# First loads in longer rows, and a new order of the transform jobs, in a Winograd convolution with batch norm

## The chip, the cores and the metric

One core of a Trainium2 chip runs the kernel. Its engines work side by side from queues of their own: TensorE (PE, with its weight loads PEld), VectorE (DVE), ScalarE (ACT), GpSimd (POOL), SyncE (SP), and 16 DMA engines that serve the DMA queues of SP and ScalarE. The metric is the device time of one execution in microseconds (us), as a median over runs.

## What is computed

Two images `x` of 2048 positions and 1024 channels are convolved along the positions with three taps, then normalised by channel and put through silu:

```python
xp = pad(x, one position on each side)
y = sum(einsum('bsc,cd->bsd', xp[:, k:k+2048], w[k]) for k in range(3))
y = silu((y - mean) * (g / sqrt(var + 1e-5)) + b)
```

All inputs and the output are bfloat16.

## The kernel before, in words

**The method.** It is a Winograd convolution: six outputs come from eight positions. Each image is cut into frames of 126 new positions (128 rows with the overlap), 16 whole ones and a short one of 48 rows. The host lays `x` out by image `bi`, block `ct` of 128 channels, row, frame and channel, so that a block is 128 rows (partitions) of 16 frames of 128 channels: 4 KB a row, 512 KB a block, eight blocks an image. The host also cuts `w` into eight groups `dc` of 128 output channels; a group has, by row, three taps of 8 x 128 values, 2 KB each.

**Stage one: transforms ("jobs").** A matmul with a frame as the loaded weights and the constant matrix `rm` (128 x 168, eight points of 21 tiles) as the moving operand transforms one frame (line 242). `Jobs.do` (237) takes 6, 6 and 4 frames of a block as three jobs; 48 jobs cover both images, in the order image, block. The results go into two banks of PSUM, and are copied to `T_sb` as bfloat16 by ScalarE (265) or VectorE (267). `do_short` (251) does the short frames of an image in one go. Below, jobs are numbered from 1 to 48 as they are issued; job 25 is the first of image 1.

**What orders it.** `ORDER` (29) is written out by hand, token by token. A capital letter is a job, and says into which two banks it goes (A 4 and 5, B 6 and 7, C 2 and 3, D 0 and 1). Small letters say which engine copies: `d` VectorE, `a` ScalarE, one letter for the whole job, two for a bank each. `s6a` is the short job into bank 6, copied by ScalarE. A bare number is so many end products: matmuls of the points 0 and infinity of the first unit (weight group 0, image 0), which use taps 0 and 2 as loaded and collect in banks 2 and 3. `p7` is so many of that unit's inner products, which use transformed weights `u`; they collect in banks 0 and 1. `m1a` makes a multiple of a tap on ScalarE; `+` issues one of the combinations on VectorE that are kept back. `COPIES` (34) says which engine copies each of the first unit's products out of PSUM. Both kinds of products are line 415; those of the later units are line 295.

**Weights.** GpSimd makes the transformed weights of a group: sums `e` (135) and then six tiles `u` (148). For group 0 it also needs three multiples (0 and 1 of the taps 2 and 0, 2 of the middle tap 1); those that have no `m` token, GpSimd makes itself (127), `FirstWeights` (165) keeps the order.

**Stage two.** 15 further units (dc, bi) run the eight products each over 342 tiles, 64 matmuls, with combinations on VectorE and silu on ScalarE. The last unit is cut in halves to shorten the end.

**Loads.** `load_x` (97) and `load_w` (105) issue from SP's queue. There are six buffers for blocks of `x`, so block 6 waits until the matmuls of block 0 are done, and so on. The program also lets each load wait for the landing of the load eight before it. In before, blocks 0 and 1 of image 0 and block 0 of image 1 come in halves by frames: 128 rows of 2 KB each. Of blocks 0 and 1 of image 0, the second half is issued from ScalarE's queue, behind `rm`. The parameters `prm` (541) are issued third from SP, and GpSimd works out scale and beta from them (217) before its first sum. Taps 0 and 2 of group 0 lie apart in the tile and come in two loads, tap 1 in a third.

Of the kernel before, what the change touches and what calls it, by code (L numbers as in the profile page):

```python
# [13 lines left out]
P = 128  # L14
# [12 lines left out]

BANKS = {"A": 4, "B": 6, "C": 2, "D": 0}
ORDER = (
    "Dda Bad Dda Cad Aad s6a Dda Cda Ada Dda 5 m1a 1 Bad Aad Da Bda Ada 2 Bda Dad Aad 1 Ba Dda 1 Ada 1 "  # L30
    "Bd 1 Dda Ada Bda 1 m2a 1 Dad Ada Ba 2 p7 Ada Cad Ba p1 Aad p3 Cad p1 Ba p1 Ada Cad p3 Bad p1 Ada p1 "
    "Cda p1 Ba p6 + Ada + p2 Cad p1 Bad Aad p2 s2a Bda p1 Ada + Cad Ba Aa"
)
COPIES = {0: "d", 7: "d", 1: "d", 3: "a", 2: "a", 5: "a"}

@with_exitstack
def kernel(
# [9 lines left out]
    nc = tc.nc  # L47
# [46 lines left out]
    def load_small(bi):  # L94
        nc.sync.dma_start(out=small[bi * SROW:bi * SROW + LROWS], in_=xl[bi])

    def load_x(bi, ct, parts=1, second=nc.scalar):
        t = xpool.tile([P, NF, P], BF16, name="xw")
        xt[bi, ct] = t
        step = NF // parts  # L100
        for q in range(parts):
            s = slice(q * step, (q + 1) * step)
            (second if q else nc.sync).dma_start(out=t[:, s], in_=x[bi, ct, :, s])

    def load_w(dc, taps):
        if dc not in raw:
            raw[dc] = wpools[dc // 2 % 2].tile([P, 3, CT, P], BF16, name=f"wch{dc // 2 % 2}")
        if len(taps) == 3:
            nc.sync.dma_start(out=raw[dc], in_=w[dc])
        else:  # L110
            for k in taps:
                nc.sync.dma_start(out=raw[dc][:, k], in_=w[dc, :, k])

# [6 lines left out]
    def scaled(src, by, eng):  # L122
        t = spool.tile([P, CT, P], BF16, name="w1x2")
        if eng is nc.scalar:
            nc.scalar.mul(t, src, by)
        else:
            eng.tensor_scalar(t, src, by, 0.0, op0=ALU.mult, op1=ALU.add)
        return t

    def double_w(dc, eng):  # L130
        double[dc] = scaled(raw[dc][:, 1], 2.0, eng)

    def even(dc, q, a, b):
        sums[dc, q] = epool.tile([P, CT, P], FP32, name=f"e{q}")
        nc.gpsimd.tensor_tensor(sums[dc, q], a, b, op=ALU.add)  # L135

    def even_vector(dc, q):
        w0, w2 = raw[dc][:, 0], raw[dc][:, 2]
        sums[dc, q] = e = epool.tile([P, CT, P], FP32, name=f"e{q}")
        f, h = (w2, w0) if q == 1 else (w0, w2)  # L140
        nc.vector.scalar_tensor_tensor(out=e, in0=f, scalar=4.0, in1=h, op0=ALU.mult, op1=ALU.add)  # L141

    def transform_w(dc, q, signs=(0, 1)):
        o = double[dc] if q else raw[dc][:, 1]
        if (dc, q) not in wts:
            wts[dc, q] = upool.tile([P, 2, CT, P], BF16, name=f"u{q}")
        for i in signs:
            nc.gpsimd.tensor_tensor(wts[dc, q][:, i], sums[dc, q], o, op=(ALU.add, ALU.subtract)[i])  # L148

    def prepare_w(dc):  # L150
        even(dc, 0, raw[dc][:, 0], raw[dc][:, 2])
        transform_w(dc, 0)

        def second():
            even_vector(dc, 1)
            transform_w(dc, 1)

        def third():
            even_vector(dc, 2)
            transform_w(dc, 2)  # L160

        act_work.append(lambda: double_w(dc, nc.scalar))
        dve_work.extend((second, third))

    class FirstWeights:
# [1 line left out]


        def __init__(self, dc):
            w0, w2 = raw[dc][:, 0], raw[dc][:, 2]  # L170
            self.dc, self.src, self.made = dc, ((w2, 4.0), (w0, 4.0), (raw[dc][:, 1], 2.0)), {}
            elsewhere = [int(t[1]) for t in ORDER.split() if t[0] == "m"]
            self.steps = [(None, lambda: even(dc, 0, w0, w2))]
            self.steps += [(i, lambda i=i: self.multiple(i, nc.gpsimd)) for i in (0,) if i not in elsewhere]
            self.steps += [(0, lambda: even(dc, 1, self.made[0], w0))]
            self.steps += [(i, lambda i=i: self.multiple(i, nc.gpsimd)) for i in (1,) if i not in elsewhere]
            self.steps += [(1, lambda: even(dc, 2, self.made[1], w2))]
            self.steps += [(i, lambda i=i: self.multiple(i, nc.gpsimd)) for i in (2,) if i not in elsewhere]
            self.steps += [
                (2 if q else None, lambda q=q, i=i: transform_w(dc, q, (i,)))  # L180
                for q, i in ((0, 0), (1, 0), (0, 1), (1, 1), (2, 0), (2, 1))
            ]
            self.own = [i for i in range(3) if i not in elsewhere]
# [8 lines left out]
                self.steps.pop(0)[1]()  # L192

    def prepare_second(dc):
        w0, w2 = raw[dc][:, 0], raw[dc][:, 2]

        def first():
            even(dc, 0, w0, w2)
            transform_w(dc, 0)

        def second():
            even(dc, 1, scaled(w2, 4.0, nc.scalar), w0)

        def third():
            double_w(dc, nc.scalar)
            transform_w(dc, 1)

        def fourth():
            even(dc, 2, scaled(w0, 4.0, nc.scalar), w2)
            transform_w(dc, 2)  # L210

        return first, second, third, fourth
# [66 lines left out]
    class Unit:  # L279
# [6 lines left out]
        def product(self, q, j, add, between):  # L286
            dc = self.dc
            nsl = slice(self.lo, self.hi)
            for ct in range(CT):
                between()  # L290
                if j == 0 or j == NJ - 1:
                    lhsT = raw[dc][:, 0 if j == 0 else 2, ct]
                else:
                    lhsT = wts[dc, (j - 1) // 2][:, (j - 1) % 2, ct]
                nc.tensor.matmul(  # L295
                    self.bank[q], lhsT=lhsT, rhs=T_sb[self.bi][:, ct, j, nsl],
                    start=not add and ct == 0, stop=ct == CT - 1, skip_group_check=add,
                )
# [90 lines left out]
    class First(Unit):  # L389
# [19 lines left out]
        def do(self, todo):  # L409
            j, q, add, ct = todo.pop(0)  # L410
            if j == 0 or j == NJ - 1:
                lhsT = raw[self.dc][:, 0 if j == 0 else 2, ct]
            else:
                lhsT = wts[self.dc, (j - 1) // 2][:, (j - 1) % 2, ct]
            nc.tensor.matmul(  # L415
                self.bank[q], lhsT=lhsT, rhs=T_sb[self.bi][:, ct, j, :],
                start=not add and ct == 0, stop=ct == CT - 1, skip_group_check=True,
            )
            if ct == CT - 1:
                self.behind(j, q)  # L420
# [115 lines left out]

    load_x(0, 0, 2)
    load_x(0, 1, 2)  # L540
    nc.sync.dma_start(out=prm, in_=prm_in)
    load_small(0)
    scales()
    nc.scalar.activation(dummy[:, 1:2], dummy[:, 0:1], ACT.Silu)
    for ct in range(2, CT):
        load_x(0, ct)
        if ct == 2:
            load_w(0, (0, 2))
    load_w(0, (1,))
    load_x(1, 0, 2, nc.sync)  # L550
    for ct in range(1, CT):
        load_x(1, ct)
    load_small(1)
    load_w(1, (0, 1, 2))

# [27 lines left out]
    prev = unit  # L585
    xscope.close()
    wpools.append(ctx.enter_context(tc.tile_pool(name="wpool1", bufs=2)))
    load_w(2, (0, 1, 2))
    load_w(3, (0, 1, 2))
    for i, (dc, bi) in enumerate(seq[1:-1], 1):  # L590
        unit = Unit(dc, bi, i % 2 * 4)
        also = prev.rest(quiet)
        if i == 1:
            also = [(1, second[0]), (4, second[1])] + also
        if i == 2:
            also = prev.rest(quiet, 5, 4)
        if i == 3:
            also = also + [(1, lambda: idle(act_work)), (1, lambda: idle(dve_work))]
        if i == len(seq) - 2:
            also = prev.rest(quiet, 4, 5)  # L600
        unit.run(
            quiet, also,
            2 if i == 2 else dc + 2 if bi == 1 and 0 < dc < DC - 2 else None, i == 2, i == 1, i == 3,
        )
        if bi == 0 and dc + 3 < DC:
            load_w(dc + 3, (0, 1, 2))
        prev.store(nc.sync)
        prev = unit

# [29 lines left out]
def _laid_out(np, x, w, mean, var, g, b):  # L639


    B, S, C = x.shape
    K, _, D = w.shape
    CT, DC = C // P, D // P
    NF = S // (R * WT)
    step = R * WT
    xp = np.zeros((B, step * NF + P, C), x.dtype)
    xp[:, 1:S + 1] = x
    wins = np.stack([xp[:, f * step:f * step + P] for f in range(NF)], 2)
    wins = wins.reshape(B, P, NF, CT, P).transpose(0, 3, 1, 2, 4)  # L650
    rm = np.zeros((P, NJ, WT), np.float32)
    for n in range(WT):
        rm[R * n:R * n + NJ, :, n] = np.array(_POINTS, np.float32).T
    return (
        wins,
        xp[:, step * NF:step * NF + LROWS],
        w.reshape(K, CT, P, DC, P).transpose(3, 2, 0, 1, 4),
        np.stack([var, g, mean, b]).reshape(4, DC, P).transpose(2, 0, 1),
        rm.astype(x.dtype),
    )  # L660
# [30 lines left out]
```

## Time and profile before

| | |
|---|---|
| median of 3 runs | 181.33 us (181.33 to 181.47) |
| the profiled execution, whole time | 181.66 us |
| its span, first to last instruction | 179.8 us |
| busy: PE, DVE, ACT, POOL | 97%, 85%, 62%, 76% of the span |
| TensorE's granted clock | 1.00 in every stretch |
| DMA engines busy, 0 to 4 us, 4 to 28 us | 45%, 100% or a little more |
| read from HBM, written | 14.93 MB, 9.44 MB |

The profile is one execution. In the timeline a row gives the start, the length from the first start to the last end, engine, line, operation and count; ends of matmuls are modelled, so a row of matmuls looks longer at its end than the pitch between them, and I go by starts. In the chain that ended last, pieces follow each other without overlap. In the table by stretch, the columns are the stretch, its length, the busy time of PE, PEld, DVE, ACT and POOL with the number of instructions, the granted clock, the mean busy share of the 16 DMA engines and the rate in GB/s; a share can exceed 1, because the time of a packet is counted from when it is taken up. Time to landing is from a load's issue to its completion.

### The profile page before, as it was taken

The page shows a single profiled execution, that of the slowest core. Times are in us where ns is not written, and L with a number is a line of the kernel's source. Part 1 is how long each engine was busy: PE and PEld are TensorE (multiplying, and loading weights), DVE is VectorE, ACT ScalarE, POOL GpSimd, SP SyncE. Part 2 cuts the span into 40 slices and gives each one's busy share as a digit, 9 for nine tenths or more (in the row PEclk, how much of TensorE's full clock was granted, in tenths as well). Part 3 has the DMA queues.
Part 4 walks back from the last instruction along what each step waited for, and adds up shares of the span by engine and source line. Part 5 has one row for each costly group of instructions (what it writes and reads, how often), then busy time and mean ns, then how long its engine had stood idle before and what let it go on. Part 6 is the DMA issues. An engine that isn't in the chain of part 4 may idle for free.

```text
span 179.8 us, 3538 instructions
## 1 busy us (share of the span) xinstructions
PE 173.9 (97%) x1365; PEld 123.2 (69%) x1365; DVE 152.2 (85%) x214; ACT 111.0 (62%) x195; POOL 137.4 (76%) x75
## 2 busy tenths in 40 slices
PE   7999999999999999999999999999999999999991
PEld 2868788766666666666666666666666666668890
DVE  1779997997969999999999999987979887766691
ACT  3799899968374847265645654555356554563773
POOL 2587999999997799999999999799799949000000
PEclk9999999999999999999999999999999999999999
DMA  5999992270335030823072306430303030203033
GB/s 172 371 416 412 418 382 109 66 289 0 131 97 213 0 131 0 232 79 131 0 195 115 133 0 135 175 133 0 135 0 131 0 125 10 97 34 137 0 155 107
DMA packets 7488, 24.58 MB, mean 137 GB/s; under 512 B 1104, under 2 KB 1616, under 8 KB 7472
## 3 DMA queue, kind: packets, MB, share of 16 engines
q1 hardware_dynamic: 6896, 23.74, 35.8%
q10 hardware_dynamic: 576, 0.63, 1.0%
q8 instruction: 10, 0.16, 0.4%
q14 instruction: 6, 0.05, 0.1%
HBM read 14.93 MB, written 9.44 MB: 136 GB/s over the span
## 4 chain that ended last, share of the span: by engine, by line
PE 87%; DMA 5%; DVE 4%; ACT 1%; issue 1%; DVEq 0%
PE ps L295 75%; PE ps L242 7%; DMA xw<-in_x_dram 5%; PE ps L415 3%; PE ps L84 2%; DVE ps L310 2%; DVE t L310 1%; DVE T_sb L267 1%; DVE sd L310 1%; ACT yh L314 1%; ACT T_sb L265 0%; ACT sd L424 0%; DVE zeros L82 0%; DVEq L680 0%; PE ps L256 0%
## 5 line engine op out<-in xcount | busy, mean ns | idle before, releaser
L295 PE MATMUL ps<-T_sb,u 128*128 128x342 bf16 (+2 forms) x768 | 109.4, 298 | 0.0
L295 PEld LDWEIGHTS <-u 128*128 128x128 bf16 x768 | 72.3, 97 | 32.6
L148 POOL TENSOR_TENSOR u<-e,w1x 128x1024 bf16<-128x1024 f32 x32 | 69.4, 2192 | 7.8 <-DVE e L141 7.6
L295 PE MATMUL ps<-T_sb,wch 128*128 128x342 bf16 (+2 forms) x256 | 39.5, 299 | 0.4 <-DVE ps L310 0.4
L310 DVE SCALAR_TENSOR_TENSOR t<-ps,sd 128x684 f32<-128x684 f32 (+2 forms) x49 | 37.6, 819 | 0.6
L148 POOL TENSOR_TENSOR u<-e,wch 128x1024 bf16<-128x1024 f32 x16 | 36.5, 2300 | 1.8 <-DMA wch<-in_w_dram 1.2
L314 ACT ACTIVATE yT<-ps,beta,scale 128x342 bf16<-128x342 f32 (+1 forms) x42 | 29.1, 727 | 12.6 <-PE ps L295 12.6
L295 PEld LDWEIGHTS <-wch 128*128 128x128 bf16 x256 | 24.2, 97 | 11.1 <-issue 0.5
L304 ACT COPY pc<-ps 128x342 f32<-128x342 f32 (+2 forms) x32 | 13.6, 424 | 28.2 <-PE ps L295 27.4
L267 DVE CAST T_sb<-ps 128x504 bf16<-128x504 f32 (+2 forms) x40 | 23.4, 644 | 5.4 <-PE ps L242 5.2
L265 ACT CAST T_sb<-ps 128x504 bf16<-128x504 f32 (+4 forms) x49 | 25.4, 597 | 3.8 <-PE ps L242 3.5
L310 DVE SCALAR_TENSOR_TENSOR ps<-ps,t 128x684 f32<-128x684 f32 (+2 forms) x32 | 26.5, 829 | 0.7
L310 DVE SCALAR_TENSOR_TENSOR ps<-ps,pc 128x342 f32<-128x342 f32 (+2 forms) x34 | 16.9, 496 | 10.1 <-PE ps L295 7.2
L141 DVE SCALAR_TENSOR_TENSOR e<-wch 128x1024 f32<-128x1024 bf16 x12 | 25.4, 2116 | 0.0
L242 PE MATMUL ps<-rm,xw 128*128 128x168 bf16 x256 | 23.8, 240 | 0.4 <-DMA xw<-in_x_dram 0.3
L242 PEld LDWEIGHTS <-xw 128*128 128x128 bf16 x256 | 20.0, 99 | 4.5 <-DMA xw<-in_x_dram 2.2
L135 POOL TENSOR_TENSOR e<-wch 128x1024 f32<-128x1024 bf16 x8 | 19.0, 2372 | 0.3 <-DMA wch<-in_w_dram 0.3
L314 ACT ACTIVATE yT<-t,beta,scale 128x684 bf16<-128x684 f32 x15 | 14.4, 959 | 0.0
L310 DVE SCALAR_TENSOR_TENSOR t<-ps,t 128x684 f32<-128x684 f32 (+2 forms) x17 | 13.9, 817 | 0.0
L304 ACT COPY sd<-ps 128x342 f32<-128x342 f32 (+2 forms) x16 | 6.8, 426 | 10.3 <-PE ps L295 9.3
L310 DVE SCALAR_TENSOR_TENSOR sd<-pc,ps 128x342 f32<-128x342 f32 (+2 forms) x17 | 8.2, 482 | 5.2 <-ACT sd L304 5.2
L306 ACT ACTIVATE pc<-ps 128x342 f32<-128x342 f32 (+2 forms) x16 | 7.0, 438 | 8.8 <-PE ps L295 5.3
(42 smaller groups left out, 66.7 us busy)
## 6 DMA issues: line engine op xcount, KB each, us to landing
out_dram<-yT SPq DMA_DIRECT2D x15, 576.0 KB, 2.9
xw<-in_x_dram SPq DMA_DIRECT2D x13, 512.0 KB, 7.2
wch<-in_w_dram SPq DMA_DIRECT2D x7, 768.0 KB, 5.4
xw<-in_x_dram SPq DMA_DIRECT2D x4, 256.0 KB, 6.7
wch<-in_w_dram SPq DMA_DIRECT2D x3, 256.0 KB, 4.5
xw<-in_x_dram ACTq DMA_DIRECT2D x2, 256.0 KB, 4.6
out_dram<-yh SPq DMA_DIRECT2D x1, 256.0 KB, 2.0
xl<-in_xl_dram SPq DMA_DIRECT2D x2, 96.0 KB, 5.2
```

The lines of the kernel that those rows point to most:

```text
L135: nc.gpsimd.tensor_tensor(sums[dc, q], a, b, op=ALU.add)
L141: nc.vector.scalar_tensor_tensor(out=e, in0=f, scalar=4.0, in1=h, op0=ALU.mult, op1=ALU.add)
L148: nc.gpsimd.tensor_tensor(wts[dc, q][:, i], sums[dc, q], o, op=(ALU.add, ALU.subtract)[i])
L242: nc.tensor.matmul(src[:, q // per, q % per], lhsT=xt[bi, ct][:, f + q], rhs=rm, start=True, stop=True)
L265: nc.scalar.copy(dst, src)
L267: nc.vector.tensor_copy(dst, src)
L295: nc.tensor.matmul(self.bank[q], lhsT=lhsT, rhs=T_sb[self.bi][:, ct, j, nsl], start=not add and ct == 0, stop=ct == CT - 1, skip_group_che ...
L304: nc.scalar.copy(dst, self.bank[q])
L306: nc.scalar.mul(dst, self.bank[q], by)
L310: nc.vector.scalar_tensor_tensor(out=out, in0=in0, scalar=scalar, in1=in1, op0=ALU.mult, op1=op1)
L314: nc.scalar.activation(self.yT[:, rows, self.y0:self.y0 + self.hi - self.lo], src, ACT.Silu, bias=beta[:, dc:dc + 1], scale=scale[:, dc:dc ...
L415: nc.tensor.matmul(self.bank[q], lhsT=lhsT, rhs=T_sb[self.bi][:, ct, j, :], start=not add and ct == 0, stop=ct == CT - 1, skip_group_check ...
```

## The change

- Blocks 0 and 1 of image 0 come in two parts of 64 rows of 4 KB instead of two halves by frames of 128 rows of 2 KB. Both parts of block 0 are issued from SP; of block 1 the second part comes from ScalarE's queue.
- The parameters are issued from ScalarE's queue, third there, behind `rm` and that part.
- Block 0 of image 1 comes in one transfer.
- The host lays the taps out as 0, 2, 1, so that taps 0 and 2 of group 0 come in one transfer, in rows of 4 KB. It is issued behind block 2 and the short block.
- `ORDER` is new. The first end products come after job 11 (after job 9 in before), 14 of the 16 before job 25 as in before. The multiple m1 has no token, so that GpSimd makes it; m2 comes after job 23 (after job 24 in before). Of the 48 inner products 28 come among the jobs (31 in before), and one combination (three in before); the rest of both follows behind the jobs. The short job of image 1 comes after job 45 (after job 43).
- `COPIES`: product 0 goes from VectorE to ScalarE, product 3 from ScalarE to VectorE.

```diff
 ORDER = (
-    "Dda Bad Dda Cad Aad s6a Dda Cda Ada Dda 5 m1a 1 Bad Aad Da Bda Ada 2 Bda Dad Aad 1 Ba Dda 1 Ada 1 "
-    "Bd 1 Dda Ada Bda 1 m2a 1 Dad Ada Ba 2 p7 Ada Cad Ba p1 Aad p3 Cad p1 Ba p1 Ada Cad p3 Bad p1 Ada p1 "
-    "Cda p1 Ba p6 + Ada + p2 Cad p1 Bad Aad p2 s2a Bda p1 Ada + Cad Ba Aa"
+    "Bad Aad Da Cda Bda Ad Da Bda s2d Aad Dad Bad 2 Aa Dda 1 Bda Aad 1 Dad 1 Bda 1 Aa 1 Dda 1 Bda 1 Ada "
+    "Dda Bad 1 m2a 2 Dd 2 Bda Aad Dda 2 Bad Aad p4 Ca p1 Bad p2 Aad Cda Ba p1 Ada p2 Ca p1 Bda p2 Aad p1 "
+    "Ca p1 Bda p1 Aa p1 Cd p2 Bad p5 + Cad Ba p4 s4a Ca Bda Aa"
 )
-COPIES = {0: "d", 7: "d", 1: "d", 3: "a", 2: "a", 5: "a"}
+
+W0, W2, W1 = range(3)
+COPIES = {0: "a", 7: "d", 1: "d", 3: "d", 2: "a", 5: "a"}
...
-    def load_x(bi, ct, parts=1, second=nc.scalar):
+    def load_x(bi, ct, parts=(nc.sync,)):
+
         t = xpool.tile([P, NF, P], BF16, name="xw")
         xt[bi, ct] = t
-        step = NF // parts
-        for q in range(parts):
+        step = P // len(parts)
+        for q, queue in enumerate(parts):
             s = slice(q * step, (q + 1) * step)
-            (second if q else nc.sync).dma_start(out=t[:, s], in_=x[bi, ct, :, s])
-
-    def load_w(dc, taps):
+            queue.dma_start(out=t[s], in_=x[bi, ct, s])
+
+    def load_w(dc, taps=slice(0, 3)):
         if dc not in raw:
             raw[dc] = wpools[dc // 2 % 2].tile([P, 3, CT, P], BF16, name=f"wch{dc // 2 % 2}")
-        if len(taps) == 3:
-            nc.sync.dma_start(out=raw[dc], in_=w[dc])
-        else:
-            for k in taps:
-                nc.sync.dma_start(out=raw[dc][:, k], in_=w[dc, :, k])
+        nc.sync.dma_start(out=raw[dc][:, taps], in_=w[dc, :, taps])
...
-    load_x(0, 0, 2)
-    load_x(0, 1, 2)
-    nc.sync.dma_start(out=prm, in_=prm_in)
+    load_x(0, 0, (nc.sync, nc.sync))
+    load_x(0, 1, (nc.sync, nc.scalar))
+    nc.scalar.dma_start(out=prm, in_=prm_in)
+    load_x(0, 2)
     load_small(0)
+    load_w(0, slice(W0, W1))
     scales()
     nc.scalar.activation(dummy[:, 1:2], dummy[:, 0:1], ACT.Silu)
-    for ct in range(2, CT):
+    for ct in range(3, CT):
         load_x(0, ct)
-        if ct == 2:
-            load_w(0, (0, 2))
-    load_w(0, (1,))
-    load_x(1, 0, 2, nc.sync)
-    for ct in range(1, CT):
+    load_w(0, slice(W1, W1 + 1))
+    for ct in range(CT):
         load_x(1, ct)
     load_small(1)
-    load_w(1, (0, 1, 2))
+    load_w(1)
...
-        w.reshape(K, CT, P, DC, P).transpose(3, 2, 0, 1, 4),
+        w[[0, 2, 1]].reshape(K, CT, P, DC, P).transpose(3, 2, 0, 1, 4),
```

Elsewhere the taps' places in the tile are named `W0`, `W2`, `W1` instead of 0, 2, 1; the instructions there are the same.

More of the change, by code (lines that the diff above doesn't have):

```diff
@@ L130, in double_w @@
     def double_w(dc, eng):
-        double[dc] = scaled(raw[dc][:, 1], 2.0, eng)
+        double[dc] = scaled(raw[dc][:, W1], 2.0, eng)
     def even(dc, q, a, b):
@@ L137, in even_vector @@
     def even_vector(dc, q):
-        w0, w2 = raw[dc][:, 0], raw[dc][:, 2]
+        w0, w2 = raw[dc][:, W0], raw[dc][:, W2]
         sums[dc, q] = e = epool.tile([P, CT, P], FP32, name=f"e{q}")
@@ L143, in transform_w @@
     def transform_w(dc, q, signs=(0, 1)):
-        o = double[dc] if q else raw[dc][:, 1]
+        o = double[dc] if q else raw[dc][:, W1]
         if (dc, q) not in wts:
@@ L150, in prepare_w @@
     def prepare_w(dc):
-        even(dc, 0, raw[dc][:, 0], raw[dc][:, 2])
+        even(dc, 0, raw[dc][:, W0], raw[dc][:, W2])
         transform_w(dc, 0)
@@ L169, in __init__ @@
         def __init__(self, dc):
-            w0, w2 = raw[dc][:, 0], raw[dc][:, 2]
-            self.dc, self.src, self.made = dc, ((w2, 4.0), (w0, 4.0), (raw[dc][:, 1], 2.0)), {}
+            w0, w2 = raw[dc][:, W0], raw[dc][:, W2]
+            self.dc, self.src, self.made = dc, ((w2, 4.0), (w0, 4.0), (raw[dc][:, W1], 2.0)), {}
             elsewhere = [int(t[1]) for t in ORDER.split() if t[0] == "m"]
@@ L194, in prepare_second @@
     def prepare_second(dc):
-        w0, w2 = raw[dc][:, 0], raw[dc][:, 2]
+        w0, w2 = raw[dc][:, W0], raw[dc][:, W2]
         def first():
@@ L291, in product @@
                 if j == 0 or j == NJ - 1:
-                    lhsT = raw[dc][:, 0 if j == 0 else 2, ct]
+                    lhsT = raw[dc][:, W0 if j == 0 else W2, ct]
                 else:
@@ L411, in do @@
             if j == 0 or j == NJ - 1:
-                lhsT = raw[self.dc][:, 0 if j == 0 else 2, ct]
+                lhsT = raw[self.dc][:, W0 if j == 0 else W2, ct]
             else:
@@ L587 @@
     wpools.append(ctx.enter_context(tc.tile_pool(name="wpool1", bufs=2)))
-    load_w(2, (0, 1, 2))
-    load_w(3, (0, 1, 2))
+    load_w(2)
+    load_w(3)
     for i, (dc, bi) in enumerate(seq[1:-1], 1):
@@ L605 @@
         if bi == 0 and dc + 3 < DC:
-            load_w(dc + 3, (0, 1, 2))
+            load_w(dc + 3)
         prev.store(nc.sync)
```

## The prediction

> **What bounds the kernel now.** I read the chain of work that ended last, in order of time, then TensorE's timeline, then the DMA rates by stretch and each load's time to landing.
>
> ```profile
> 4.48 2.96 PE ps L242 x28
> 7.44 0.32 PE ps L256 x8
> 7.75 1.77 PE ps L242 x20
> 9.52 0.02 issue
> 9.54 9.25 DMA xw<-in_x_dram
> 18.79 0.05 issue
> 18.84 1.40 PE ps L242 x16
> ...
> 37.51 126.54 PE ps L295 x872
> ```
>
> Columns are start, length, what. From 18.84 us on TensorE carries the chain almost alone, and 126.54/872 = 145 ns a matmul from 37.51 on leaves no gap. Ahead of that stands one load, issued at 9.54: the first half of image 1's block 0. So the run's end is set by when that block lands, plus TensorE's work, plus its gaps between there and 37.5. Nothing after 37.5 is touched by the change.
>
> The gaps after 18.84: to 37.35 (start of the pure L295 stretch) are 18.51 us. The work is 128 transform matmuls at 72.5 ns (six take 0.43 us), 50 products of L415 at 145 ns (three take 0.43), eight of L295 and 0.24 for the short block: 9.28 + 7.25 + 1.16 + 0.24 = 17.93. **0.58 us is lost.** The largest piece is visible here:
>
> ```profile
> 31.35 0.84 PE L242 MATMUL ps<-rm,xw 128*128 128x168 bf16 x6
> 32.02 0.31 PE L415 MATMUL ps<-T_sb,u 128*128 128x342 bf16 x1
> ```
>
> Six matmuls need 0.435 us, and the next starts 0.67 after them: 0.235 waiting for a bank to be copied out. (VectorE had stood 1.0 us behind ScalarE's copy of sd, by the table of waits.)
>
> The DMA rates by stretch (length, busy time of PE, PEld, DVE, ACT and POOL, clock, DMA share, GB/s):
>
> ```profile
> 1.75:3.75 2.00, 2.00 (x4) 0.76 (x3) 0.08 (x1) 1.49 (x2) 0.00 (x0) 1.00 0.76 240
> 3.75:5.75 2.00, 2.00 (x11) 1.10 (x10) 0.68 (x1) 0.26 (x1) 0.00 (x0) 1.00 1.09 359
> 7.00:8.50 1.50, 1.50 (x25) 1.18 (x23) 1.50 (x3) 1.50 (x5) 1.34 (x3) 1.00 1.03 395
> 8.50:14.50 6.00, 5.59 (x62) 4.36 (x60) 4.94 (x10) 5.64 (x12) 5.36 (x6) 1.00 1.03 415
> 25.50:27.00 1.50, 1.50 (x19) 1.26 (x17) 1.40 (x4) 1.50 (x4) 1.50 (x2) 1.00 1.03 347
> 34.75:36.75 2.00, 2.00 (x15) 1.33 (x14) 1.97 (x4) 2.00 (x4) 2.00 (x2) 1.00 0.88 292
> ```
>
> From 4 to 28 us the DMA engines are full, so a load lands when the bytes ahead of it have moved. It runs 415 GB/s on 4 KB rows, 395 where the 2 KB rows of taps 0 and 2 pass, and less in the first four microseconds.
>
> **The change, part by part.**
>
> *Block 0 of image 1 in one transfer.* Its halves were issued at 9.54 and 9.92 and took 9.3 and 9.5 us, so they land at 18.84 and 19.42. The first job needs the whole block now: **+0.58**. (Jobs on the first half covered this before.)
>
> *Rows of 4 KB.* First two microseconds of the stream: 240 GB/s with 2 KB rows. The nearest row with longer rows is the weight load that starts at 34.75, with 6 KB rows, 292 in its first two microseconds. The difference is 0.104 MB, at 415 0.25 us. From 3.75 to 5.75 it is 359 against 415, 0.11 MB or 0.27 us; in 5.25 to 5.75 (331 and 279 GB/s in its quarters) the short block and the parameters pass, which stay, and that is 0.13 of it; between 0.14 and 0.27 I take 0.20, since the parameters leave SP's queue. Taps 0 and 2 (0.52 MB) at 415 for 395: 0.06; block 0 of image 1 alike: 0.06. Sum **-0.57**; bounds 0 and -0.64, and above zero by the first rival.
>
> *Image 0's first job later.* It used frames 0 to 5, in the first 256 KB, which landed at 0.72 + 3.5 = 4.22, when the warm-up matmuls (to 4.48) still ran. Now it needs all of block 0. SP's queue had moved 0.49 MB by 4.25, and its first two loads had landed by 1.16 + 4.2 = 5.36, so I expect the start near 5. What hides it: block 3 lands at 5.67 + 5.3 = 10.97, and the nine jobs ahead of it need 48 x 72.5 ns + 0.3 = 3.8 us. Cost nothing up to two microseconds of delay.
>
> *The six end products moved behind block 3.* They filled 9.65 to 11.0. Now TensorE must do 80 transforms (5.8 us) and 14 end products (2.03) between block 3 of image 0 and block 0 of image 1: 7.83 us, where 19.42 - 10.97 = 8.45 are there. Slack 0.62. Cost nothing while the DMA gain at block 0 of image 1 isn't over 0.62 more than at block 3. Copying out in that stretch: VectorE 10 x 0.59 + 0.76 + 2 x 0.42 = 7.5, ScalarE 10 x 0.47 + 2 x 0.61 + 2 x 0.34 = 6.6, as before (pitches from neighbouring casts in the two timelines); it fits.
>
> *Queues.* SP issues the parameters no more, and one load for two taps; each issue is 0.33 to 0.43 us. The waits of SP's queue show 1.4 us until the first load (rm) landed ahead of the ninth, and that order stays: the pair of taps is still ninth. By then 1.7 MB are queued and 0.75 moved, so earlier issues gain nothing. On ScalarE one issue of 0.45 comes before its table load (2.12 to 3.40), whose first copy is due after 5: nothing. GpSimd needs the parameters for 3.05 us of scales (6.10 to 9.15) ahead of its first sum at 9.49, which waits for the taps: 0.3 us of cover. If they land later, its u tiles do, and u0 (20.35) is first read 2.3 us after block 0 of image 1: a microsecond of cover more.
>
> *The multiple m1 from ScalarE to GpSimd.* ScalarE -1.08; GpSimd +1.04, beside its 1.2 us wait for tap 1 (17.0 to 18.23): hidden to within 0.2. *m2* stands one job earlier: ScalarE reaches it 7.5 us after block 3, tap 1 lands 7.2 after (18.2): no wait.
>
> *Jobs of image 1.* Loads of the engines from block 0 of image 1 to the last job, copies and combinations included, by the same pitches (VectorE's small operations 0.42, ScalarE's 0.35, a whole job of 1008 on ScalarE 0.90):
>
> | us | TensorE | VectorE | ScalarE |
> |---|---|---|---|
> | before | 14.3 | 13.1 | 13.1 |
> | after | 13.9 | 11.4 | 13.6 |
>
> Laid out by hand, each copy 0.2 us behind its matmuls and each bank refilled when it is empty, the new order leaves TensorE two gaps, 0.04 ahead of job 35 and 0.1 where VectorE's combination waits for ScalarE's copy of sd ahead of job 46. The copies of jobs 46 to 48 end 1.4 us after the last job, beside 12 products (1.74). So 0.14 of gaps for 0.58: **-0.44**. Bounds 0 (a layout by hand sees no jitter) and -0.58.
>
> Sum: +0.58 - 0.57 - 0.44 = **-0.43**. The profiled execution took 181.66 us (span 179.8), 0.33 above the median of the runs, 181.33; I take the difference over to the median: **180.90**. A difference under 0.2%, 0.36 us, is about what a measurement of this kernel can't tell from none.
>
> **A row that speaks against it.** Where the short block of image 1 passes (48 rows, 25.5 to 27.0), the rate is 347: 0.10 MB is missing for 0.10 MB of such rows, though the engines are busy. In 5.25 to 5.5, where the other short block passes, the share is 1.63 at 331 GB/s. Transfers that span fewer rows ran at about half rate here. [...]
>
> **Rivals.**
>
> *Parts of 64 rows run at half rate* (slower). By the rows above, half of 415 is 208. Part one runs alone at a time that gave only 170 GB/s anyway (1.75 to 2.75). Then the second part of block 0 on SP and of block 1 on ScalarE's queue share the same rows 64 to 127: until about 4.95; then the first part of block 1, 0.26 MB at 208, to about 6.15, where the same bytes had moved by 5.45 before. The stream is 0.7 late: +0.58 - 0.12 - 0.44 + 0.7 = +0.72, **182.05**; all four in series, 5.0 us from 1.75 (6.8 for 5.4), make 1.4 and 182.75. It decides from the point where the stream is late at all: without the 0.45 of gain on the first four microseconds the sum is +0.02. For: the rows of the short blocks. Against: those are of 2 KB and 48 rows, and two queues can mix parts.
>
> *Copying out takes the place of the wait* (same or slower). ScalarE has 13.6 us in a stage of 13.9. One wait like the 1.0 us of VectorE in before, less the 0.3 of slack, costs 0.7: -0.43 + 0.7 = +0.27, **181.6**; with the old 0.58 of gaps **181.3**, two waits 182.6.
>
> *The slowest DMA engine* (faster). Tap 1 lands at 18.2, 2.2 us after block 7 (8.18 + 7.8 = 15.98), though 256 KB take 0.63. In 15.2 to 16.2 one packet of instructions held an engine for 6% of 16 us, 0.96 us, and every later load waits for that engine. If it comes later, block 0 of image 1 lands up to 0.96 earlier; then TensorE's 7.83 us bind, at 10.97 - 0.51 + 7.83 = 18.29 for 19.42 - 0.57 = 18.85: 0.56 more, **180.35**. Against: its time goes with the instructions done, nearly the same here.
>
> *The rows of 4 KB bring nothing*: +0.57 on the sum, +0.14, **181.5**, counted within the forecast's own spread.
>
> **Chances.** Forecast 0.42 (its own range 180.7 to 181.4; 0.27 faster, 0.13 same, 0.02 slower); slow DMA engine 0.19, all faster; copying out 0.11 (0.05 same, 0.06 slower); half rate 0.28 (0.02 same, 0.26 slower). Faster 0.46, same 0.20, slower 0.34. The range leaves out the half rate in series and the extreme of the fast side: 180.3 to 182.1.
>
> **What will show it.** Right: about 290 GB/s or more in the first two microseconds of the stream; first transform near 5; block 0 of image 1 starting at about 18.85 in one stretch; the pure L295 stretch from about 36.9. Half rate: 200 GB/s and a share over 1 in 2 to 6 us, block 3 after 11. Copying out: block 0 early, but gaps of TensorE behind ScalarE in 20 to 34. The forecast is wrong if block 0 of image 1 starts after 19.3.

## The result, and the profile after

| | before | after |
|---|---|---|
| median, runs side by side | 181.34 us | 183.08 us (182.85 to 183.49) |
| ratio after / before | | 1.0097, 95% interval 1.0076 to 1.0119 |
| the profiled execution, whole time | 181.66 us | 183.28 us |
| its span | 179.8 us | 181.2 us |
| job 25 starts | 18.84 us | 20.62 us |
| from there to the pure stretch of products | 18.51 us | 18.10 us |
| pure stretch starts | 37.35 us | 38.72 us |
| from there to the end of the span | 142.45 us | 142.48 us |

The change made the kernel slower by 1.74 us; 180.90 was forecast, and the range ended at 182.1. The line numbers fall by one in the code of the jobs: 241, 414 and 294 are what 242, 415 and 295 were.

The table splits the difference of the profiled executions. Job 25, the first of image 1, starts 1.78 us later. The stage behind it is 0.41 shorter. The rest is the same to 0.03. So all of the loss happened before 20.6 us.

The chain that ended last, in order of time (start, length, what), of the kernel after:

```profile
1.34 5.51 DMA xw<-in_x_dram
6.85 0.14 issue
6.98 5.02 PE ps L241 x44
12.00 0.32 PE ps L255 x8
12.32 1.27 PE ps L241 x16
...
20.32 0.29 PE ps L414 x2
20.61 0.02 issue
20.62 1.33 PE ps L241 x16
```

In before this chain hung on one load that was issued at 9.54. Now it begins with the first block: its second part, issued at 1.34 and landed at 6.85. From 6.98 TensorE never pauses until job 25. And its first 44 transforms take 5.02 us, 114 ns each, where those of before came 72.5 ns apart from 6.04 to 7.20. (Before began slowly too: its first 28 took 2.96 us, 106 ns each, a wait of about 0.2 us included.)

The same stretches as before, from the table by stretch (stretch, length, busy time of PE, PEld, DVE, ACT and POOL, granted clock, DMA share, GB/s), with two more that turned out to matter:

```profile
1.75:3.75 2.00, 2.00 (x4) 0.75 (x3) 0.08 (x1) 1.41 (x2) 0.00 (x0) 1.00 0.78 218
3.75:5.75 2.00, 0.72 (x2) 0.00 (x0) 0.00 (x0) 0.08 (x1) 0.00 (x0) 1.00 1.07 220
5.75:7.25 1.50, 0.27 (x4) 0.30 (x5) 0.00 (x0) 0.00 (x0) 0.00 (x0) 1.00 1.06 201
8.50:11.50 3.00, 3.00 (x24) 3.00 (x22) 2.48 (x4) 1.77 (x4) 2.54 (x6) 0.50 1.02 354
```

Two things are to be seen. Between 3.75 and 7.25 the DMA engines are full (share over 1) and yet move 220 and 201 GB/s, where before moved 359 and 380 in the same two stretches. And from 8.5 to 11.5 TensorE runs at half its clock (0.50), with 24 matmuls recorded in 3 us.

### The profile page after: what moved, and what is told of

It is laid out like the page before. It is cut to its first block, busy times and chain, and to the rows that moved or that the text cites. A ratio compares the mean times of both kernels' runs of the same rounds, so it can differ in the third digit from the quotient of the medians.

```text
span 181.2 us, 3533 instructions
## 1 busy us (share of the span) xinstructions
PE 173.6 (96%) x1365; PEld 124.4 (69%) x1365; DVE 148.9 (82%) x211; ACT 110.3 (61%) x191; POOL 139.6 (77%) x76
## 4 chain that ended last, share of the span: by engine, by line
PE 91%; DMA 3%; DVE 3%; ACT 1%; SPq 0%; issue 0%; DVEq 0%
PE ps L294 74%; PE ps L241 12%; PE ps L414 5%; DMA xw<-in_x_dram 3%; DVE ps L309 2%; DVE t L309 1%; ACT yh L313 1%; SPq L106 0%; PE ps L255 0%; DVEq L678 0%; DVE sd L309 0%; PE ps L612 0%; DVEq L309 0%
## 5 line engine op out<-in xcount | busy, mean ns | idle before, releaser
L147 POOL TENSOR_TENSOR u<-e,w1x 128x1024 bf16<-128x1024 f32 x32 | 70.4, 2223 | 6.3 <-DVE e L140 4.9
L147 POOL TENSOR_TENSOR u<-e,wch 128x1024 bf16<-128x1024 f32 x16 | 35.7, 2249 | 0.6
L266 DVE CAST T_sb<-ps 128x504 bf16<-128x504 f32 (+3 forms) x37 | 22.9, 665 | 8.3 <-PE ps L241 7.4
L241 PE MATMUL ps<-rm,xw 128*128 128x168 bf16 x256 | 24.5, 246 | 2.5 <-DMA xw<-in_x_dram 2.5
L241 PEld LDWEIGHTS <-xw 128*128 128x128 bf16 x256 | 21.2, 102 | 5.9 <-issue 3.7
L140 DVE SCALAR_TENSOR_TENSOR e<-wch 128x1024 f32<-128x1024 bf16 x12 | 22.0, 1835 | 0.0
L134 POOL TENSOR_TENSOR e<-wch 128x1024 f32<-128x1024 bf16 x8 | 20.0, 2495 | 0.2 <-DMA wch<-in_w_dram 0.2
```

The lines of the kernel that those rows point to most:

```text
L241: nc.tensor.matmul(src[:, q // per, q % per], lhsT=xt[bi, ct][:, f + q], rhs=rm, start=True, stop=True)
L266: nc.vector.tensor_copy(dst, src)
```

## The experiments

The first theory was that the parts of 64 rows move at half rate, and that the late stream alone sets the end. The rivals were that the late first job and the clock it cost set it, or the order of the two queues, or the parameters. Each kernel ran beside the kernel before, whose median was 181.31, 181.33 and 181.25 us on the three chips used. Each row of a table below stands on one profiled execution, and each ratio on the runs.

### The parts of 64 rows taken away, and by themselves

First the kernel after, with blocks 0 and 1 in one transfer each:

```diff
-    load_x(0, 0, (nc.sync, nc.sync))
-    load_x(0, 1, (nc.sync, nc.scalar))
+    load_x(0, 0)
+    load_x(0, 1)
```

> The changed kernel with blocks 0 and 1 of image 0 each in one transfer of 128 rows of 4 KB from SP; all else as changed. Theory A (a part of 64 neighbouring rows moves at half rate, about 205 GB/s for 415): the stream runs above 350 GB/s from 3 us on, block 0 of image 1 lands near 18.9 instead of 20.6, and the time is 180.8 to 181.3. Theory B (only TensorE's idle 2.5 us and its half clock from 8.0 to 11.5 cost time): the time also falls, because block 0 of image 0 lands earlier, but the rate in 4 to 7 us stays near 205. Theory C (the cost is in the new job order): no gain, 183.

Measured: **180.60 us**, ratio 0.9964 (0.9952 to 0.9976). It beats both kernels, and by a little more than was expected. Its table by stretch:

```profile
1.75:3.75 2.00, 2.00 (x4) 0.75 (x3) 0.08 (x1) 1.37 (x2) 0.00 (x0) 1.00 0.77 268
3.75:5.75 2.00, 1.79 (x17) 1.16 (x16) 0.43 (x1) 0.66 (x2) 0.00 (x0) 1.00 1.05 407
```

Same bytes, same rows of 4 KB, same share: 407 GB/s for 220. Job 25 starts at 18.28.

Then the other way round, the kernel before with nothing changed but these four parts:

```diff
-    load_x(0, 0, 2)
-    load_x(0, 1, 2)
+    load_rows(0, 0, (nc.sync, nc.sync))
+    load_rows(0, 1, (nc.sync, nc.scalar))
```

> The kernel before, in its old order, with one thing changed: blocks 0 and 1 of image 0 in parts of 64 rows of 4 KB on the queues of the change (SP, SP; SP, ScalarE). If these parts alone carry the loss: about 205 GB/s in 4 to 7 us, the first half of block 0 of image 1 near 20.3 for 18.84, time 182.6 to 183.2. If the loss needs the rest of the change too: 181.3 to 181.8.

Measured: **184.14 us**, ratio 1.0165 (1.0129 to 1.0201). Two lines of its TensorE timeline (start, length, what, and in brackets the idle time ahead; the second is the beginning of job 25) and two of its table by stretch:

```profile
6.60 3.77 PE L250 MATMUL ps<-rm,xw 128*128 128x168 bf16 x28 [2.12 <-DMA xw<-in_x_dram]
...
20.92 0.30 PE L250 MATMUL ps<-rm,xw 128*128 128x168 bf16 x2
```

```profile
3.75:5.75 2.00, 0.73 (x2) 0.00 (x0) 0.00 (x0) 0.00 (x0) 0.00 (x0) 1.00 1.06 240
5.75:7.25 1.50, 0.65 (x6) 0.69 (x6) 0.04 (x1) 0.00 (x0) 0.00 (x0) 1.00 1.13 216
```

The parts alone bring the half rate, the late first transform (6.60 for 4.45), a slow TensorE behind it (28 transforms in 3.7 us, 132 ns each) and 2.9 us. Removed they give back 2.5. They are the cause. The way by which they reach the end was not the expected one here, though, and the loss is larger than expected: the first half of block 0 of image 1 was to land near 20.3, but it landed at 18.14, earlier than in before (18.79). Job 25 started at 20.92, 2.08 later than in before, and no wait stands ahead of it. So in this kernel TensorE's late and slow start, with the copies that hang on it, set job 25 alone; the data were long there.

What a packet costs is read from the list of DMA queues in half a microsecond (packets, MB, share of the 16 engines), first of the kernel after in 4.75 to 5.25, then of whole blocks in 4.0 to 4.5:

```profile
q1 hardware_dynamic: 24, 0.10, 95.7%
```

```profile
q1 hardware_dynamic: 50, 0.20, 97.5%
```

16 engines x 0.5 us x 0.957 / 24 is 319 ns a packet of 4 KB, for 156 ns in whole blocks. The engines' shares are about the same, 95.7% and 97.5%; each packet takes twice as long. The trace shows the longer packets and not what they wait for.

### The queues

Of the kernel after, both second parts from ScalarE's queue, and in another kernel all four parts from SP's:

```diff
-    load_x(0, 0, (nc.sync, nc.sync))
+    load_x(0, 0, (nc.sync, nc.scalar))
```

> The changed kernel with the second part (rows 64 to 127) of both blocks from ScalarE's queue, so that lower and upper rows are in flight together from two queues. If half rate comes from the rows that a part covers and the queues mix: lower and upper parts share the engines, rate above 300 GB/s, block 0 of image 1 at 19 to 19.6, time 181.2 to 181.9. If two parts on two queues still go one after the other at the engines: rate about 210, time 183.

Measured: **184.40 us**, ratio 1.0175 (1.0160 to 1.0190). The rate rose only to 250 and 265 GB/s in 3.75 to 5.75 and 5.75 to 7.25. The parameters, now behind two parts, arrived 1.7 us later than in after, and TensorE waited 0.7 for a `u` tile. The chain that ended last goes through the parameters and GpSimd. So this run doesn't tell what the small gain in rate would have brought, and neither expected time, 181.2 to 181.9 or 183, came.

```diff
-    load_x(0, 1, (nc.sync, nc.scalar))
+    load_x(0, 1, (nc.sync, nc.sync))
```

> The changed kernel with all four parts of 64 rows issued from SP, in order, so that nothing of block 1 overtakes block 0. Theory A (half rate binds): block 0 of image 0 lands near 5.3 instead of 6.85 and TensorE keeps its clock, but the stream still runs at about 205 GB/s until 7, block 0 of image 1 lands at 20 to 20.6, time 182.4 to 183.1. If the order of the two queues was the main loss: block 0 of image 1 near 19, time under 181.6.

Measured: **182.90 us**, ratio 1.0091 (1.0071 to 1.0111). In after, ScalarE's part of block 1 was issued at 1.14, SP's second part of block 0 at 1.34; ScalarE's landed at 5.55, the other, needed first, at 6.85. With one queue TensorE starts a microsecond earlier, at 5.95. It is no better for it: the 44 transforms take 5.4 us, and the chain that ended last goes through block 3, landed at 12.10, and TensorE's 8.15 us from there to job 25, at 20.25. Block 0 of image 1 landed at 20.21, so the data came no earlier than TensorE was ready. The order of the queues makes the first job later, but it isn't what sets the end.

### The clock

Of the kernel after, warm-up matmuls that last until about 6:

```diff
-    for _ in range(2):
-        nc.tensor.matmul(ps[:, 3, 0:416], lhsT=zeros[:, 0:P], rhs=zeros, start=True, stop=True)
+    for n in (416, 416, 416, 208):
+        nc.tensor.matmul(ps[:, 3, 0:n], lhsT=zeros[:, 0:P], rhs=zeros[:, 0:n], start=True, stop=True)
```

> The changed kernel with the warm-up of TensorE made longer: three matmuls of 416 columns and one of 208 instead of two of 416, so that it ends near 6.9 instead of 4.5 and TensorE hardly idles before its first transform. Theory A (the late loads bind: block 0 of image 1 lands at 20.6): the clock stays full and the first 44 transforms take 3.2 instead of 5.0 us, but job 25 still starts near 20.6, time 182.8 to 183.1. Theory B (TensorE's half clock is what costs): job 25 starts 1.5 to 1.8 earlier, time 181.3 to 181.6.

Measured: **182.91 us**, ratio 1.0089 (1.0074 to 1.0104). TensorE was idle for 0.86 us instead of 2.51, and the 44 transforms took 3.7 us instead of 5.0. The granted clock goes with it. In after it stands at 1.00 from 4.74 to 8.16, a stretch of which TensorE worked only 1.2 us, and at 0.50 from there to 11.57: the first 16 transforms behind the idle time still came 72 ns apart, the following 24 came 140 apart. With the longer warm-up it reads 1.00 from 8.5 to 11.5, where it read 0.50 in after. The chain of this kernel shows what took over:

```profile
11.28 9.16 DMA xw<-in_x_dram
...
38.71 126.54 PE ps L294 x872
```

Now the load of block 0 of image 1 ends the wait, at 20.44. In after it had landed at 20.55 and TensorE was ready at 20.61: both chains ended together, so that the cure of one shows the other.

### Parts that reach all rows

Parts of every second row span all 128 rows:

```diff
-            s = slice(q * step, (q + 1) * step)
+            s = slice(q, P, len(parts))
```

> The changed kernel, but each of the two parts of blocks 0 and 1 takes every second row (even rows, odd rows) instead of the lower and the upper 64. Number, size and queue of the transfers are the same. [...] Theory A2 (it matters that a part has only 64 rows, so 4 packets an engine): rate and time stay, about 205 GB/s and 183.1.

Measured: **182.61 us**, ratio 1.0066 (1.0039 to 1.0093), where 183.1 was expected if it is the number of a part's rows that counts. The rates were 231 and 364 GB/s from 3.75 to 5.75 and from 5.75 to 7.25, for 220 and 201 in after. Block 0 of image 1 landed at 18.4, early; but the first transform began at 6.60, and 44 transforms took 5.13 us. Here TensorE's slow pace set job 25, at 20.27.

The early landing is in part chance. Tap 1, ahead of that block, landed 0.8 earlier than in after (17.2 for 18.0). The rest goes with a packet of instructions that took 1.01 us of one DMA engine in after and 0.97 in before (the prediction's rival "the slowest DMA engine"); that it delays the loads behind it is inferred from the landings. In after it starts at 17.76, and block 0 lands 2.6 us behind tap 1; here it starts at 17.93, block 0 lands 1.2 us behind tap 1, and block 1 behind it takes the delay (2.3 us).

So both cures together:

```diff
-    for _ in range(2):
...
+    for n in (416, 416, 416, 208):
...
-            s = slice(q * step, (q + 1) * step)
+            s = slice(q, P, len(parts))
```

> Both cures in one: parts of every second row (block 0 of image 1 landed at 18.5 with them) and the longer warm-up. If two things each hold the time up alone, the late stream and TensorE's late and slow start, the time falls now where each cure alone left 182.6 and 182.9: block 3 of image 0 lands at 11.6, TensorE needs 7.8 us from there, job 25 near 19.4, time 181.3 to 181.7. If TensorE's clock has no part in it: 182.6 as without the warm-up.

Measured: **182.00 us**, ratio 1.0046 (1.0029 to 1.0062), well above the 181.3 to 181.7 expected. Job 25 starts at 19.10, which is better by 1.5 than after, but not the 18.3 of whole blocks. Block 0 of image 1 took the delay of the packet of instructions again, 2.4 us behind tap 1, and landed at 19.05. Parts of every second row are not full speed: 236 GB/s in 3.75 to 5.75 at a share of 0.90. Some DMA engines stood idle in the first microseconds; why is not settled.

### A part by itself

The kernel before, with nine more loads (one of them as two halves) into a tile that nothing reads, one in each quiet stretch of the later units (ScalarE's queue), two of them whole blocks, the others parts:

```diff
+    def whole():
+        nc.scalar.dma_start(out=probe, in_=x[1, 0])
...
+    def upper():
+        nc.scalar.dma_start(out=probe[64:128], in_=x[1, 2, 64:128])
...
+    probes = {4: whole, 5: lower, 6: upper, 7: short_rows, 8: even_rows, 9: quarter, 10: both, 11: whole, 12: lower}
```

> The kernel before with nine extra loads from ScalarE's queue into a tile that nothing reads, each in the middle of a later unit when the DMA engines are idle: a whole block (128 rows of 4 KB), rows 0 to 63, rows 64 to 127, 128 rows of 2 KB, every second row, rows 0 to 31, both halves one behind the other, and the first two again. If half the rows mean half the rate: a packet of 4 KB takes about 160 ns in the whole block and 320 ns in rows 0 to 63 or 64 to 127 alone, so 256 KB move in as long as 512 KB do, and rows 0 to 31 run no slower than rows 0 to 63. If the loss belongs to the start of the program alone: 160 ns in all of them. Its own time is not compared.

A single run took 181.37 us. A whole block of 512 KB landed 3.2 and 3.3 us after its issue. Rows 64 to 127, 256 KB, took 3.5, and rows 0 to 63 as long: a half takes as long as the whole. Every second row took 2.9. (Three of the nine met weight loads and tell nothing.) The DMA queue in the middle half microsecond of a whole block, and of rows 64 to 127:

```profile
q10 hardware_dynamic: 51, 0.21, 103.3%
```

```profile
q10 hardware_dynamic: 26, 0.11, 74.4%
```

162 ns a packet against 229. Both halves behind each other moved 213, 295, 270 and 180 GB/s, at up to 266 ns a packet. The slower packet is there by itself, but not the 319 ns of the start. The rate is nearly the same, though: 26 packets in the half microsecond here (213 GB/s) and 24 at the start (197). The difference lies in the share, 74.4% and 95.7%: at the start more engines held a packet at the same time, and each packet lasted longer. So the rate is about halved in both places, while a packet took 229 ns beside a share of 74.4% and 319 beside 95.7%; where the halving itself comes from, the trace doesn't show. TensorE's and the other engines' work has no part in the 319 ns, since they stood still in 4.5 to 6.9.

### Halves by frames, and the parameters

Could the parts be kept by cutting along frames, as in before? All 128 rows, 2 KB each:

```diff
-        step = P // len(parts)
+        step = NF // len(parts)
...
-            queue.dma_start(out=t[s], in_=x[bi, ct, s])
+            queue.dma_start(out=t[:, s], in_=x[bi, ct, :, s])
...
-    load_x(0, 0, (nc.sync, nc.sync))
+    load_x(0, 0, (nc.sync, nc.scalar))
```

> The changed kernel with blocks 0 and 1 of image 0 in halves by frames as before (128 rows of 2 KB, second halves from ScalarE's queue), all else as changed. Against whole blocks of 4 KB rows (180.6, block 0 of image 1 at 18.26) it prices the length of the rows. By the prediction's rates (0.25 and 0.20 us for the first four microseconds) block 0 of image 1 lands at 18.7 to 19.0, time 181.0 to 181.3. If row length is worth nothing: 180.6.

Measured: **182.90 us**, ratio 1.0092 (1.0073 to 1.0111), where 181.0 to 181.3 was expected. The rates were 380 and 395 GB/s, and yet it was slow. Two lines of its timeline, GpSimd's and TensorE's:

```profile
8.77 0.20 POOL L220 TENSOR_SCALAR sc<-prm 128x8 f32<-128x8 bf16 x1 [7.21 <-DMA prm<-in_prm_dram]
```

```profile
22.80 0.76 PE L414 MATMUL ps<-T_sb,u 128*128 128x342 bf16 x4 [0.91 <-ACT T_sb L264]
```

GpSimd waited 7.21 us for the parameters, and its first `u` tile was ready only at 22.75. TensorE stood 0.91 ahead of the first product that reads it. The row names a copy of ScalarE, which ended at 22.79: both came together, so the profile alone doesn't say which of them counted. Hence the same kernel with the parameters back on SP's queue, behind block 1:

```diff
-    nc.scalar.dma_start(out=prm, in_=prm_in)
+    nc.sync.dma_start(out=prm, in_=prm_in)
```

> The changed kernel with halves by frames (182.9) and the parameters back on SP's queue behind block 1. GpSimd there waited for them until 8.77, and its first weight tile reached TensorE 0.9 us late. If the parameters behind ScalarE's loads cost that: GpSimd starts near 6, no wait of TensorE for the tile, time 181.6 to 182.1. If not: 182.9.

Measured: **181.76 us**, ratio 1.0025 (1.0015 to 1.0034). Job 25 comes at 19.23 for 19.40, and the stage behind it takes 18.11 us for 19.17: the late parameters had cost 1.1 us there. In after they also came late (8.05 for 6.10), but the taps landed only at 11.23, and GpSimd would have waited for those anyway.

### Order and loads, one at a time

The kernel before with the new `ORDER` and `COPIES`, old loads:

```diff
-    "Dda Bad Dda Cad Aad s6a Dda Cda Ada Dda 5 m1a 1 Bad Aad Da Bda Ada 2 Bda Dad Aad 1 Ba Dda 1 Ada 1 "
+    "Bad Aad Da Cda Bda Ad Da Bda s2d Aad Dad Bad 2 Aa Dda 1 Bda Aad 1 Dad 1 Bda 1 Aa 1 Dda 1 Bda 1 Ada "
...
-COPIES = {0: "d", 7: "d", 1: "d", 3: "a", 2: "a", 5: "a"}
+COPIES = {0: "a", 7: "d", 1: "d", 3: "d", 2: "a", 5: "a"}
```

> The kernel before with the new order of the jobs and the new table of copies alone; loads as before, block 0 of image 1 in halves. The prediction's step: TensorE needs 7.83 us from block 3 (10.97), so job 25 starts at 18.8 to 18.9, and from there to the pure stretch it takes 18.1 instead of 18.51 us: time 180.8 to 181.0. If the order is worth nothing with the old loads: 181.3. If the wait for block 3 without end products to fill it costs more than reckoned: above 181.5.

Measured: **181.35 us**, ratio 1.0003 (0.9991 to 1.0015): no gain in the runs, where 180.8 to 181.0 was expected. Then the loads of the first experiment with the old `ORDER` and `COPIES`:

```diff
-    "Bad Aad Da Cda Bda Ad Da Bda s2d Aad Dad Bad 2 Aa Dda 1 Bda Aad 1 Dad 1 Bda 1 Aa 1 Dda 1 Bda 1 Ada "
+    "Dda Bad Dda Cad Aad s6a Dda Cda Ada Dda 5 m1a 1 Bad Aad Da Bda Ada 2 Bda Dad Aad 1 Ba Dda 1 Ada 1 "
...
-    load_x(0, 0, (nc.sync, nc.sync))
-    load_x(0, 1, (nc.sync, nc.scalar))
+    load_x(0, 0)
+    load_x(0, 1)
```

> The loads of the fastest kernel so far (whole blocks of 4 KB rows, taps 0 and 2 in one, parameters on ScalarE's queue: 180.6) under the old order of the jobs and the old table of copies. The new order alone, on the old loads, gave nothing (181.35). If the loads are the whole gain: 180.5 to 180.8. If it takes both, since the old order has gaps of its own: 181.0 to 181.4.

Measured: **181.16 us**, ratio 0.9998 (0.9988 to 1.0007). With the first experiment this makes a table of four:

| | old order | new order |
|---|---|---|
| old loads | 181.25 to 181.33 | 181.35 |
| whole blocks in 4 KB rows | 181.16 | 180.60 |

Neither half can be told from nothing, and both together bring 0.7 us. The profiled executions show why they need each other (job 25 starts, stage behind it): loads alone 18.28 and 18.53, order alone 18.77 and 18.09, both 18.28 and 18.09. The new order shortens the stage by 0.4 with either loads. But it puts the six end products behind block 3, so that job 25 hangs on that block. In the order alone the first half of block 0 of image 1 had landed at 17.1, and job 25 waited for TensorE, whose chain runs without a pause from block 3 (10.82) to 18.77. Whole blocks bring block 3 at 10.21, and with it job 25 at 18.28.

In the profile each half looks half a microsecond better than before (pure stretch at 36.86 and 36.81 for 37.35), and the runs show next to nothing of it. That is the reference: the profiled execution of before, with a span of 179.8 us, was a long one. The spans of before's runs beside these two kernels have a median of 179.4; those of order alone and of loads alone have 179.35. By that median, job 25 of a usual execution of before starts at an estimated 18.4 (179.4 less 142.45 and 18.51): what the new order gains in the stage it loses ahead of it, as long as block 3 comes no earlier.

## Why the prediction was wrong, point by point

- **"Rows of 4 KB", -0.57: the step that failed.** It priced all loads at the rate of whole blocks, 415 GB/s. The four parts moved 0.20 to 0.22 MB a microsecond at full engines, and block 0 of image 1 landed at 20.55 instead of 18.85. That alone is +1.70. With it the prediction's own sum, -0.43, becomes +1.27; the profile shows +1.37 at the pure stretch, and the runs 1.74. For whole blocks the term had the right sign and half the size: 268 and 407 GB/s for 240 and 359 (+28 x 2 us and +48 x 2 us, 0.15 MB or 0.37 us at 415, of 0.45 reckoned for these stretches), and yet block 0 of image 1 landed at 18.26, 1.16 before the 19.42 of its second half in before. That is 0.59 more than the term. It was not tried by itself, but the landings show that most of it came early: block 3 was already 0.76 ahead (10.21 for 10.97) and block 7 0.85 (15.14 for 15.99).
- **The rival "half rate" was the case.** It stood in the prediction with 0.28 and two prices, 182.05 with the parts overlapping and 182.75 with all four in series. 183.08 is beyond the second. It had the row (the short blocks), and its signs came: 220 and 201 GB/s at a share over 1 from 3.75 to 7.25, and block 3 at 12.40, 1.43 later than in before, as the 1.4 in series. The argument set against it, that two queues can mix parts, is answered: on two queues the rate was 250 to 265. The range was cut at 182.1, short of the price in series, which was a likely form and not an extreme.
- **"Cost nothing up to two microseconds of delay": failed too.** The first transform came 2.5 us late, at 6.98 for 4.48, and not near 5, since ScalarE's part overtook the one that was needed. And a price was missing: behind 2.51 us of idle time TensorE's clock stood at 0.50 for 3.41 us (8.16 to 11.57), and the 44 transforms that take 3.19 us at 72.5 ns took 5.02. The table of before, with a clock of 1.00 in every stretch, gave no warning: the first record of its clock starts at 5.97, the table reads 1.00 ahead of it too, and most of its transforms up to there start 140 ns apart. TensorE was thus ready for job 25 at 20.61. This is a second way from the same parts to the end, beside the first and not on top of it: the load came at 20.55 in any case. With the idle time cured the run took 182.91, with parts that reach all rows 182.61, with both 182.00.
- **Block 0 of image 1 in one transfer, +0.58.** Not measured by itself. Whole blocks at 18.28 show that it costs nothing that the earlier stream doesn't cover.
- **"TensorE must do ... 7.83 us"** from block 3 to job 25: measured 8.07 with whole blocks (10.21 to 18.28) and 8.15 with one queue. The small difference matters, since with whole blocks the data came at 18.26 and TensorE was ready at the same time: its slack of 0.62 was gone.
- **The new order, -0.44: right in the profile** (18.10 for 18.51, -0.41; 18.09 in two other kernels). Its value in the runs hangs on the loads: 0.56 us with early ones (181.16 to 180.60), none with the old ones.
- **The rival "slowest DMA engine"** did not come. In after the packet of instructions started at 17.76, and block 0 of image 1 landed 2.6 us behind tap 1; in before it started at 15.84, and tap 1, ahead of that block, landed 2.2 us behind block 7. In the rows alone (18.33), with every second row (17.93) and in the order alone (16.59) it came too late to delay the data of job 25, but there TensorE set job 25.
- **Copying out** was no bound: 18.10 us of stage against 17.93 of work leave 0.17 of gaps, for 0.14 reckoned.
- **The parameters, "nothing": right for this kernel, and for another reason.** They came 1.95 us later, far over the cover of 0.3; but the taps, slowed by the same parts, came at 11.23, when the scales were just done (11.10). Where the loads are fast and ScalarE's queue carries two halves, it costs 1.1 us.
- **"Each issue is 0.33 to 0.43 us": too low for the parts.** A part of 64 rows took SP 0.57 to 0.61, and the whole block right behind them 0.59. SP issued the short block's load at 3.26, for 2.08 with whole blocks. The DMA engines' share was 1.07 from 3.75 to 5.75 all the same, so this was hidden.

## What to carry to other kernels

Keep all 128 rows in each transfer, and don't cut a first load without need: here a half of the rows took as long as the whole (256 KB in 3.5 us, 512 KB in 3.2 and 3.3), and whole blocks (180.60) were better than halves along the free axis (181.76 at best). Engines that look busy can hide a low rate (220 GB/s at a share of 1.07 here, 407 at 1.05 with whole blocks), so read share and GB/s together. A delay that slack covers can still cost: here TensorE stood still for 2.51 us in it, its clock then read 0.50 for 3.41, and 44 transforms took 5.02 us for 3.19. Where two chains end within 0.1 us of each other, the cure of one shows next to nothing, so they are to be cured together and one by one. An order of work and an arrival time can be worth something only jointly: price them as a pair. And compare a profile with more than one execution of the kernel before: the span of the one here was 0.4 us longer than the median of the runs.

## What the runs showed of the hardware

- A packet of 4 KB took 319 ns in parts of 64 neighbouring rows at the start of the program and 156 ns in whole blocks, with all 16 DMA engines busy in both. In a quiet stretch it took 229 ns at a share of 74.4%, and the rate was halved all the same (213 GB/s, for 418 in a whole block).
- Two queues with parts of opposite halves raised the rate from 201 to 220 up to 250 to 265 GB/s, about a fifth, still far from the 407 and 374 of whole blocks in the same stretches.
- ScalarE's part of block 1, issued at 1.14, was served nearly alone: from 3.25 to 4.25 us its queue had 101% of the engines' time and SP's 5%, although SP's second part of block 0 had been issued only 0.2 us later.
- In after TensorE's granted clock stood at 1.00 from 4.74 to 8.16 us, a stretch of which TensorE worked 1.2, and at 0.50 from 8.16 to 11.57. The change shows in the starts of the transforms, 72 and 140 ns apart, and it came 1.2 us after the idle time of 2.51 had ended. With two queues, where TensorE was idle for 1.17 us ahead of 5.65 and for 1.43 ahead of 8.40, the clock read 0.50 from 8.5 to 11.5 too, and 28 transforms took 3.76 us; with the longer warm-up, behind 0.86 us, it read 1.00. Three kernels don't show what lowers the clock.
- A granted clock of 1.00 in the table is no proof. In the rows alone, with every second row and with one queue it reads 1.00 in each microsecond from 6.5 to 12.5, and yet TensorE has only 9 or 10 matmuls in each of those from 7.5 to 9.5, and 17 to 20 in the one from 10.5. So the slow transforms of these kernels, behind idle time of 2.12, 2.12 and 1.47 us, stand beside no lower clock in the table; why they were slow is not shown. The pace of the rows is the safer reading.
